# Filter convolution and SiLU layer: the first batch's products in rounds of two frequency pairs, with shared PSUM banks and two more groups in front of the second part

## Chip, cores and metric

One Trainium2 chip, one core, one launch. The metric is device time in microseconds (us), the median of the runs.

## The reference

```python
# batch 2, seq 12480, d_model 128, filter_order 64, d_ff 2048; all float32
h = maximum(pos_emb @ w1, 0) @ w2 * exp(-0.01 * pos)[:, None]     # the filter
u = x * v
y = irfft(rfft(u, 2*S) * rfft(h, 2*S))[:, :S]                     # causal convolution
a = (x * y).reshape(B*S, D)
g = a @ w_in;  out = (g * sigmoid(g)) @ w_out
```

## The kernel before

The transform is split by hand into two stages. A sequence is laid out as 98 x 64 points in two halves. Stage A turns the 98 points of a column into 98 frequencies by a matrix product; of these, frequencies come in 49 pairs q (NQ = 49). The second stage, for each pair, transforms over the 64 columns, multiplies by the filter's spectrum and transforms back, and its result `ws` goes to device memory (`wd`), from where tiles of tokens are loaded, transformed back over the 98 points (`yp`), multiplied with x (`ring`) and fed to the second part, the SiLU layer.

The kernel is scheduled by hand: each engine runs its instructions in the order in which the program writes them, and waits on what it reads. Its stretches:

- First stretch (string `seq`, a letter for each step): the filter's network, stage A of the filter (`Xh`) and of the first batch (`X`), the weights' conversion. The letters `f` and `B` load the first matrices and make the first filter products (`hp`).
- The loop over the 49 pairs (L661 to L694), first batch. For a pair q: `u_step` (L597) makes `up` on TensorE and ACT copies it, the halves exchanged, to `uw`. `hb_step` (L301) makes `hp`, the filter's transform of pair q + 3, which ACT copies to `zt`; `spectrum` (L321) makes `sps` of pair q + 1 from it, which ACT copies to `hab`. DVE multiplies `up` by parts of `hab` in place (`a_early`, `a_late`, with the temporary `at`), POOL does the like on `uw` (`b_step`, result `bt`), DVE adds both into `ps` (`s_step`). Two iterations later `w_step` (L645) makes `wps` from `ps`; ACT and DVE turn it into `ws` (`even_odd`), and SP stores it. `hab` is also stored (`hs`), for the second batch. `hp` has a PSUM pool of its own (`php`), `up` two buffers of one bank, `sps` and `wps` two banks each, whose halves two successive pairs use in turn.
- `side_steps` (L553), called in each iteration, does work beside the loop: it loads and splits the converted weights into high and low parts (L547 on ACT, L551 on DVE), loads and multiplies the first two groups of the second batch (L270 on POOL), and in iteration 47 loads further groups into `slots`.
- The bridge (string `seq3`): the last pairs' products, stage A of the second batch's first four groups (`stage_a_pairs`, L234: sixteen TensorE instructions into a tile `ap` of two banks, then four copies into X, all on ACT for `A`, on DVE for `a`), an activation table load, weight splits (`h`, `l`), the load of the first token tile (`L`) and its products (`Y`).
- The second part (from L961): the SiLU layer over 49 spans of tokens in 784 steps of six products, and beside it, paced by a counter, stage A of the remaining 28 groups of the second batch and then its products.

Of the kernel before, what the change touches and what calls it, by code (L numbers as in the profile page):

```python
# [31 lines left out]
NQ = R // 2  # L32
RE = 128
# [32 lines left out]
def moe_tiles():  # L66
# [15 lines left out]
    x47=2,  # L82
# [7 lines left out]
    seq3='smAumULASahhllhhllaxxrrrrYLxhhllhhll',  # L90
# [4 lines left out]
def kernel(  # L95
# [17 lines left out]
    fb0: bass.AP,  # L113
# [120 lines left out]
    def stage_a_pairs(g, psp, us, bufs, on_act):  # L234

        ap = psp.tile([128, 2, 512], F32, name=f"ap1_{g}", tag="ap", bufs=bufs)
        for k in range(4):
            for e in range(2):
                r = slice(64 * e, 64 * e + NQ)
                nc.tensor.matmul(ap[:, e, R * k : R * k + R], us[r, k], fe_sb[r], start=True, stop=True)  # L240
        for i in range(NI):
            for c in range(2):
                src = ap[64 * i : 64 * i + 64, :, 0 : 4 * R].rearrange("p e (d c q) -> p c q e d", c=2, q=NQ)
                dst = X[64 * c : 64 * c + 64, :, i * D + 4 * g : i * D + 4 * g + 4]
                dst = dst.rearrange("p (q e) d -> p q e d", e=2)
                if on_act:
                    nc.scalar.copy(out=dst, in_=src[:, c])
                else:
                    nc.vector.tensor_copy(dst, src[:, c])
# [44 lines left out]
    def load_fb(src, rp, q, bufs, e):  # L294
        t = rp.tile([128, 2, 2, 128], F32, name=f"fb{q}", tag="fb", bufs=bufs)
        e.dma_start(out=t, in_=src[q])
        return t

    fbs, zs, habs, prods = {}, {}, {}, {}

    def hb_step(q):  # L301

        if php is None:
            hp = psa.tile([128, 4, 256], F32, name=f"hp{q}", tag="ap", bufs=4)[:, 0]
            hp = hp.rearrange("p (k c n) -> p k c n", k=2, c=2)
        else:
            hp = php.tile([128, 2, 2, 64], F32, name=f"hp{q}", tag="hp", bufs=2)
        for k in range(2):
            for s in range(2):
                r = slice(64 * s, 64 * s + 64)  # L310
                nc.tensor.matmul(  # L311
                    hp[r, k].rearrange("p c k -> p (c k)"),
                    Xh[2 * q >= KA][:, 2 * q - (2 * q >= KA) * KA + k, r],
                    fbs[q][:, k, 0],
                    start=True,
                    stop=True,
                )
        zs[q] = rpa.tile([128, 2, 2, 64], F32, name=f"zt{q}", tag="zt", bufs=3)
        nc.scalar.copy(out=zs[q], in_=hp)

    def spectrum(q, hab):  # L321

        zt = zs.pop(q)
        sp = sps[:, :, q % 2]
        for m in range(2):
            for s in range(2):
                r = slice(64 * s, 64 * s + 64)
                for k in range(2):
                    nc.tensor.matmul(sp[64 * k : 64 * k + 64, s, m], zt[r, k, m], w2_sb[r], start=True, stop=True)  # L329
        nc.scalar.copy(out=hab.rearrange("p m s d -> p s m d"), in_=sp)  # L330
# [69 lines left out]
    php = None  # L400
    n_a = n_z = n_h = n_f = 0
# [9 lines left out]
    for t in P["seq"]:  # L411
# [35 lines left out]
        elif t == "|":  # L447
            early.release()
            xpool = pool("xpool")
            X = xpool.tile([128, R, NI * D], F32, name="X")  # L450
            rpa = pool("rp2a")
        elif t == "f":
            fbs[n_f] = load_fb(fb0, rpa, n_f, 4, nc.sync)
            n_f += 1
        elif t == "B":
            hb_step(len(zs))
# [7 lines left out]
    php = pool("php", space=PSUM, side="right")  # L464
# [57 lines left out]
    def even_odd(b, q, rp, wp, nb):  # L522

        p, tag, n = (rp, "ws", nb["ws"]) if b or q < NQ - 2 else (rp, "fb", 9)
        ws = p.tile([128, NI, 2, D], F32, name=f"ws{b}_{q}", tag=tag, bufs=n)
# [66 lines left out]
    nb = dict(up=2, uw=2, at=2, bt=2, ps=2, ws=2)  # L592

# [3 lines left out]
    def u_step(q):  # L597

        up = pp.tile([128, 2, NI, D], F32, name=f"up0_{q}", tag="up", bufs=nb["up"])
        for c in range(2):  # L600
            for k in range(2):
                nc.tensor.matmul(  # L602
                    up[64 * k : 64 * k + 64, c].rearrange("p i d -> p (i d)"),
                    fbs[q][:, k, 0, 64 * c : 64 * c + 64],
                    X[:, 2 * q + k],
                    start=True,
                    stop=True,
                )
        uw = rp.tile([128, 2, NI, D], F32, name=f"uw0_{q}", tag="uw", bufs=nb["uw"])
        nc.scalar.activation(out=uw[:, 0], in_=up[:, 1], func=AF.Copy, scale=-1.0)  # L610
        nc.scalar.copy(out=uw[:, 1], in_=up[:, 0])  # L611
        return up, uw

    def times_h(e, out, u, h):
        e.tensor_tensor(out=out, in0=u, in1=h.unsqueeze(1).broadcast_to([128, u.shape[1], D]), op=ALU.mult)  # L615

    def flat(t):
        return t.rearrange("p c i d -> p (c i) d")
# [4 lines left out]
    def a_early(q, up, hab):  # L623
        a2 = rp.tile([128, 2, D], F32, name=f"at{q}", tag="at", bufs=nb["at"])
        times_h(nc.vector, a2, up[:, :, 0], hab[:, 0, 1])
        return a2

    def a_late(up, hab, a2):
        times_h(nc.vector, flat(up), flat(up), hab[:, 0, 0])
        add(nc.vector, up[:, :, 1], up[:, :, 1], a2)  # L630

    def b_step(q, uw, hab):
        bt = rp.tile([128, 3, 2, D], F32, name=f"bt{q}", tag="bt", bufs=nb["bt"])
        b01 = bt[:, 0:2]
        times_h(nc.gpsimd, flat(b01), flat(uw), hab[:, 1, 0])
        times_h(nc.gpsimd, bt[:, 2], uw[:, :, 0], hab[:, 1, 1])
        add(nc.gpsimd, b01[:, :, 1], b01[:, :, 1], bt[:, 2])
        return b01

    def s_step(q):  # L640
        up, bt = prods[q]
        prods[q] = rp.tile([128, 2, NI * D], F32, name=f"ps{q}", tag="ps", bufs=nb["ps"])
        add(nc.vector, prods[q].rearrange("p c (i d) -> p c i d", i=NI), up, bt)

    def w_step(q):  # L645

        p, f = prods.pop(q), fbs.pop(q)
        wp = wps[:, :, q % 2]
        for c in range(2):
            for k in range(2):  # L650
                r = slice(64 * k, 64 * k + 64)
                nc.tensor.matmul(wp[:, k], f[r, c, 1], p[r, c], start=(c == 0), stop=(c == 1))  # L652
        wss[q] = even_odd(0, q, rp, wp.rearrange("p k (i d) -> p k i d", i=NI), nb)
        next(wss[q])

    def ws_step(q):
        for _ in wss.pop(q):
            pass

    wss = {}  # L660
    for it in range(-1, NQ):  # L661
        while n_f <= min(it + 6, NQ - 1):
            fbs[n_f] = load_fb(fb0, rp, n_f, 9, nc.sync if it < 0 else nc.scalar)
            n_f += 1
        q = it
        if 0 <= q < NQ:
            up, uw = u_step(q)
        q = it - 3
        if 0 <= q < NQ:
            ws_step(q)  # L670
        q = it
        if 0 <= q < NQ:
            a2 = a_early(q, up, habs[q])
        q = it - 1
        if 0 <= q < NQ:
            s_step(q)
        q = it + 3
        if 3 <= q < NQ:
            hb_step(q)
        q = it + 1  # L680
        if 0 <= q < NQ:
            hab = rp.tile([128, 2, 2, D], F32, name=f"hab{q}", tag="hab", bufs=3)
            spectrum(q, hab)
            habs[q] = hab
        q = it
        if 0 <= q < NQ:
            hab = habs.pop(q)
            a_late(up, hab, a2)
            prods[q] = up, b_step(q, uw, hab)
            nc.sync.dma_start(out=hs[q], in_=hab.rearrange("p m s d -> p (m s d)"))  # L690
        q = it - 2
        if 0 <= q < NQ:
            w_step(q)
        side_steps(it)  # L694

    pps.release()
    php.release()
    psa = pool("psa3", space=PSUM)
# [17 lines left out]
    def attn_tile(n, wt, xs, psp, tag):  # L716
# [3 lines left out]
        yp = psp.tile([128, 512], F32, name=f"yp{n}", tag=tag[0], bufs=tag[1])  # L720
# [34 lines left out]
    n_a = n_t = n_h = n_l = 0  # L755
    n_r = 4
    for t in P["seq3"]:
# [69 lines left out]
    def batch1_steps():  # L827
        for g in range(NA, D // 4):
            uv.mul(nc.gpsimd)
            yield P['ya']  # L830
            stage_a_pairs(g, psa, uss.pop(g), 1, True)
# [7 lines left out]
        def load_f(q):  # L839
            return load_fb(fb, rp, q, 2, nc.sync)  # L840
# [186 lines left out]
def _constants():  # L1027
# [23 lines left out]
    fb0 = np.stack([fwd, inv0], axis=1).reshape(NQ, 2, 2, 128, 128).transpose(0, 3, 1, 2, 4)  # L1051
# [5 lines left out]
    return {k: np.ascontiguousarray(a, dtype=np.float32) for k, a in dict(fa=fa, fs=fs, feo=feo, fe=fe, fb=fb, fb0=fb0, win=win).items()}  # L1057
# [56 lines left out]
```

## Time and profile before

| | |
|---|---|
| median of 3 runs | 1545.48 us (1542.5 to 1547.77) |
| the profiled execution | 1546.87 us, of which the trace spans 1545.0 |
| TensorE (PE) busy | 1514.3 us, 98% |
| VectorE (DVE) / ScalarE (ACT) / GpSimd (POOL) busy | 1227.3 / 990.2 / 633.5 us |
| chain that ended last | 91% on PE |
| first stretch, loop, bridge, second part | to 109.5, to 262.4, to 281.4, to 1545 us |

PE is the matrix engine, PEld its weight loads, SP the queue that issues most transfers. A busy PE is not one that streams at its peak: an instruction's record covers its latency too, and records overlap. So the order and the distance of the starts tell more than the busy share.

### The profile page before, as it was taken

The numbers are of one execution on the slowest core, as the hardware profiler recorded it, in microseconds if no ns is written. First come the engines' busy times: TensorE is split into PE (matmuls) and PEld (weight loads), VectorE is DVE, ScalarE is ACT, GpSimd is POOL, SyncE is SP. The second block draws the span as 40 slices with busy tenths as digits, with TensorE's granted clock in tenths as the row PEclk, the third lists the DMA queues.
The fourth block names the chain that finished last, engine by engine and source line by source line (L and its number), as shares of the span: only waits on it lengthen the run. The fifth ranks groups of instructions, "written<-read, shape, count | busy, mean of one in ns | idle before, by whom it ended". The sixth has DMA issues, their size and how long they took to land.

```text
span 1545.0 us, 31519 instructions
## 1 busy us (share of the span) xinstructions
PE 1514.3 (98%) x11732; PEld 1245.1 (81%) x11732; DVE 1227.3 (79%) x2138; ACT 990.2 (64%) x1910; POOL 633.5 (41%) x671
## 2 busy tenths in 40 slices
PE   8989998899999999999999999999999999999999
PEld 7976666787888888888888888888888888888887
DVE  5658898676799999999999987777777777777776
ACT  2545665677778788787887765555555555555554
POOL 3658888233378888888888730000000000000000
PEclk9999999799999999999999999999999999999999
DMA  8767787654354454544445521111111211111100
GB/s 238 215 211 240 254 291 243 197 167 145 99 150 137 132 148 143 143 137 142 142 142 155 147 89 38 46 47 40 47 41 47 62 34 46 54 33 47 53 30 14
DMA packets 115569, 184.84 MB, mean 120 GB/s; under 512 B 11058, under 2 KB 48984, under 8 KB 115416
## 3 DMA queue, kind: packets, MB, share of 16 engines
q1 hardware_dynamic: 101368, 158.45, 33.9%
q10 hardware_dynamic: 14048, 24.37, 4.8%
q8 instruction: 93, 1.52, 0.4%
q14 instruction: 60, 0.49, 0.1%
HBM read 129.37 MB, written 53.41 MB: 118 GB/s over the span
## 4 chain that ended last, share of the span: by engine, by line
PE 91%; DVE 3%; DMA 2%; ACT 1%; issue 1%; POOL 1%; ACTq 0%; SPq 0%; DVEq 0%; POOLq 0%
PE op L1001 12%; PE hq L968 11%; PE hq L969 11%; PE op L1002 11%; PE hq L970 11%; PE op L1003 11%; PE yp L727 4%; PE wps L652 3%; PE up L602 3%; PE ap L218 2%; PE wp L471 2%; PE aph L379 2%; PE ap L240 2%; PE up L471 2%; PE sps L329 2%; PE hp L311 1%
## 5 line engine op out<-in xcount | busy, mean ns | idle before, releaser
L975 ACT ACTIVATE g<-hq 128x512 f32<-128x512 f32 x424 | 253.9, 599 | 265.2 <-PE hq L970 237.4
L980 DVE TENSOR_TENSOR gl<-g,gh 128x512 fp32r<-128x512 f32 x424 | 293.6, 692 | 94.5 <-PE hq L970 65.8
L1001 PE MATMUL op<-gh,woh 128*128 128x512 f32 (+1 forms) x784 | 313.3, 400 | 0.0
L968 PE MATMUL hq<-ah,wih 128*128 128x512 f32 (+1 forms) x784 | 308.2, 393 | 2.0 <-ACT ah L749 1.3
L969 PE MATMUL hq<-al,wih 128*128 128x512 f32 (+1 forms) x784 | 306.1, 390 | 0.7 <-DVE al L751 0.7
L1002 PE MATMUL op<-gl,woh 128*128 128x512 f32 (+1 forms) x784 | 305.8, 390 | 0.0
L970 PE MATMUL hq<-ah,wil 128*128 128x512 f32 (+1 forms) x784 | 305.7, 390 | 0.0
L1003 PE MATMUL op<-gh,wol 128*128 128x512 f32 (+1 forms) x784 | 305.1, 389 | 0.0
L975 ACT ACTIVATE hq<-hq 128x512 f32<-128x512 f32 (+1 forms) x360 | 206.7, 577 | 95.2 <-PE hq L970 85.5
L980 DVE TENSOR_TENSOR gl<-hq,gh 128x512 fp32r<-128x512 f32 (+1 forms) x360 | 243.9, 683 | 22.5 <-ACT gh L979 13.5
L977 DVE CAST gh<-hq 128x512 fp32r<-128x512 f32 (+1 forms) x247 | 166.3, 673 | 41.7 <-ACT hq L975 41.2
L977 DVE CAST gh<-g 128x512 fp32r<-128x512 f32 x318 | 135.1, 425 | 72.1 <-ACT g L975 71.7
L968 PEld LDWEIGHTS hq<-ah,wih 128*128 128x128 f32 x784 | 147.9, 189 | 39.2 <-DVE gl L980 6.6
L970 PEld LDWEIGHTS hq<-ah,wil 128*128 128x128 f32 x784 | 148.0, 189 | 31.1
L969 PEld LDWEIGHTS hq<-al,wih 128*128 128x128 f32 x784 | 148.0, 189 | 30.3 <-DVE al L751 1.1
L1003 PEld LDWEIGHTS op<-gh,wol 128*128 128x128 f32 x784 | 147.5, 188 | 30.7
L1001 PEld LDWEIGHTS op<-gh,woh 128*128 128x128 f32 x784 | 147.7, 188 | 29.5 <-issue 0.2
L1002 PEld LDWEIGHTS op<-gl,woh 128*128 128x128 f32 x784 | 147.9, 189 | 24.3 <-DVE gl L980 0.3
L615 POOL TENSOR_TENSOR bt<-uw,hab 128x512 f32<-128x512 f32 x98 | 96.2, 1004 | 17.8 <-ACT uw L611 17.5
L727 PEld LDWEIGHTS yp<-feo_sb,slots 98*64 98x64 f32 x2048 | 64.9, 139 | 21.5 <-issue 17.7
L727 PE MATMUL yp<-feo_sb,slots 98*64 98x49 f32 (+1 forms) x2048 | 71.4, 225 | 3.3 <-DMA slots<-wd 3.3
L270 POOL TENSOR_TENSOR slots<-slots 128x512 f32<-128x512 f32 x30 | 39.0, 1300 | 84.6 <-DMA slots<-in_ve_dram 71.9
(1065 smaller groups left out, 2405.9 us busy)
## 6 DMA issues: line engine op xcount, KB each, us to landing
slots<-hs SPq DMA_DIRECT2D x98, 256.0 KB
slots<-wd SPq DMA_DIRECT2D x48, 490.0 KB
hs<-hab SPq DMA_DIRECT2D x49, 256.0 KB
wd<-ws SPq DMA_DIRECT2D x49, 256.0 KB
slots<-in_fb_dram SPq DMA_DIRECT2D x49, 256.0 KB
wd<-slots SPq DMA_DIRECT2D x49, 256.0 KB
out_dram<-ot ACTq DMA_DIRECT2D x48, 256.0 KB
fb<-in_fb_dram ACTq DMA_DIRECT2D x43, 256.0 KB
```

The lines of the kernel that those rows point to most:

```text
L471: nc.tensor.matmul(out[:, k].rearrange("p i d -> p (i d)"), f[:, k], a[:, k], start=(i == 0), stop=(i == len(passes) - 1),)
L615: e.tensor_tensor(out=out, in0=u, in1=h.unsqueeze(1).broadcast_to([128, u.shape[1], D]), op=ALU.mult)
L727: nc.tensor.matmul(yp[h : h + 64, a : a + k], wt[:, t, e * D + h : e * D + h + 64], feo_sb[:, e, 0:k], start=True, stop=True,)
L968: nc.tensor.matmul(hp[:, 0:w], wih[:, fs], ah[:, 0:w], start=True, stop=False)
L969: nc.tensor.matmul(hp[:, 0:w], wih[:, fs], al[:, 0:w], start=False, stop=False)
L970: nc.tensor.matmul(hp[:, 0:w], wil[:, fs], ah[:, 0:w], start=False, stop=True)
L975: nc.scalar.activation(out=g[:, 0:w], in_=hp[:, 0:w], func=AF.Silu)
L977: nc.vector.tensor_copy(gh[:, 0:w], g[:, 0:w])
L980: nc.vector.tensor_tensor(out=gl[:, 0:w], in0=g[:, 0:w], in1=gh[:, 0:w].bitcast(F32), op=ALU.subtract)
L1001: nc.tensor.matmul(o[:, 0:w], woh[:, fs], gh[:, 0:w], start=(f == 0), stop=False)
L1002: nc.tensor.matmul(o[:, 0:w], woh[:, fs], gl[:, 0:w], start=False, stop=False)
L1003: nc.tensor.matmul(o[:, 0:w], wol[:, fs], gh[:, 0:w], start=False, stop=(f == NF - 1))
```

## The change

The loop takes two pairs in one round (25 rounds, the last with one pair). Each tile of the loop is twice as large and most have one buffer instead of two or three; one vector instruction does for two pairs what two did, but the copies to `uw` and `hab`, and two of the products on POOL, stay one for a pair. The filter's products `hp` of the next round are written into one of the two banks of `sps`, in front of that round's `up`. The forward and inverse matrices are loaded separately (`ff`, `fi`). In the bridge six groups instead of four go through stage A, in turn into a tile of their own and into the buffers of `up`, one of them (`b`) with half of its copies on ACT and half on DVE; the second part has 26 groups left, four instead of two are loaded in iteration 47, and `side_steps` starts three iterations earlier.

```diff
-    x47=2,
+    x47=4,
-    seq3='smAumULASahhllhhllaxxrrrrYLxhhllhhll',
+    seq3='sbmULAmSamAmahhllhhllxxrrrrYLxhhllhhll',
@@ stage_a_pairs
-                if on_act:
+                if on_act[i]:
@@
+    def load_ff(r, e):
+        ffs[r] = rpa.tile([128, 2, 2, 128], F32, name=f"ff{r}", tag="ff", bufs=4)
+        e.dma_start(out=ffs[r], in_=ff[r])
+    def load_fi(r, e):
+        fis[r] = rp.tile([128, 2, 2, 128], F32, name=f"fi{r}", tag="fi", bufs=3)
+        e.dma_start(out=fis[r], in_=fi[r])
+    def qs(r):
+        return range(min(2, NQ - 2 * r))
-    def hb_step(q):
...
+    def hp_mm(hp, r, n):            # four products of pair 2r + n into hp
...
+    def zt_tile(r):
+        zs[r] = rpa.tile([128, 2, 2, 2, 64], F32, name=f"zt{r}", tag="zt", bufs=2)
+    def spectrum(r, hab):
+        zt = zs.pop(r)
+        for n in qs(r):
...
+                        nc.tensor.matmul(
+                            sps[64 * k : 64 * k + 64, s, n, m], zt[h, n, k, m], w2_sb[h], start=True, stop=True
+                        )
+        for n in qs(r):
+            nc.scalar.copy(out=hab[:, n].rearrange("p m s d -> p s m d"), in_=sps[:, :, n])
@@ side_steps
-        k = it - (KA // 2 + 1)
+        k = it - (KA // 2 - 2)
@@
+    def u_step(r):
+        up = pp.tile([128, 2, 2, NI, D], F32, name=f"up0_{r}", tag="up", bufs=2)
+        uw = rp.tile([128, 2, 2, NI, D], F32, name=f"uw0_{r}", tag="uw", bufs=1)
+        for n in qs(r):
...
+            nc.scalar.activation(out=uw[:, n, 0], in_=up[:, n, 1], func=AF.Copy, scale=-1.0)
+            nc.scalar.copy(out=uw[:, n, 1], in_=up[:, n, 0])
+    def a_step(r, up, hab):         # at has bufs=1
...
+        times_h(nc.vector, a2, up[:, :, :, 0], hab[:, :, 0, 1])
+        times_h(nc.vector, flat(up), flat(up), hab[:, :, 0, 0])
+        add(nc.vector, u1, u1, a2.rearrange("p n c d -> p (n c) d"))
+    def b_step(r, uw, hab):         # bt has bufs=2, b2 bufs=1
...
+        for n in range(w):
+            k = slice(n, n + 1)
+            times_h(nc.gpsimd, flat(bt[:, k]), flat(uw[:, k]), hab[:, k, 1, 0])
+        times_h(nc.gpsimd, b2, uw[:, :, :, 0], hab[:, :, 1, 1])
+        add(nc.gpsimd, b1, b1, b2.rearrange("p n c d -> p (n c) d"))
+    def s_step(r):                  # one addition for the round; ps has bufs=1
+    def w_step(r):                  # both pairs' products, one ACT copy to ws
+    def ws_step(r):                 # two DVE instructions, one store to wd
+    def ap_tile(g):
+        return (psa, "ap", 1) if g % 2 == 0 else (pp, "up", 2)
@@ the loop
+    for r in range(-1, NR):
+        # loads of ff (three rounds ahead) and fi (one ahead), on ACT's queue from r = 0
+        if r >= 2:
+            ws_step(r - 2)
+        if 1 <= r + 1 < NR:
+            hp = sps[:, 0].rearrange("p n m d -> p (n m d)").rearrange("p (n k c t) -> p n k c t", n=2, k=2, c=2)
+            for n in qs(r + 1):
+                hp_mm(hp[:, n], r + 1, n)
+            nc.scalar.copy(out=zt_tile(r + 1)[:, 0:w], in_=hp[:, 0:w])
+        if r >= 1:
+            s_step(r - 1)
+        if r >= 0:
+            up, uw = u_step(r)
+        if r + 1 < NR:
+            habs[r + 1] = rp.tile([128, 2, 2, 2, D], F32, name=f"hab{r + 1}", tag="hab", bufs=2)
+            spectrum(r + 1, habs[r + 1])
+        if r >= 0:
+            a_step(r, up, hab)
+            prods[r] = up, b_step(r, uw, hab)
+            # store of hab to hs
+        if r == NR - 1:
+            pps.release()
+            psa = pool("psa3", space=PSUM)
+            stage_a_pairs(0, *ap_tile(0), uss.pop(0), (True, True))
+        if r >= 1:
+            w_step(r - 1)
+        for it in (2 * r, 2 * r + 1):
+            if 0 <= it < NQ:
+                side_steps(it)
@@ the bridge
+    n_a = 1
+            on_act = {"A": (True, True), "a": (False, False), "b": (True, False)}[t]
+            stage_a_pairs(n_a, *ap_tile(n_a), uss.pop(n_a), on_act)
         elif t == "s":
+            s_step(NR - 1)
+            ws_step(NR - 2)
         elif t == "U":
+            w_step(NR - 1)
+            ws_step(NR - 1)
```

In the first stretch two matrices `ff` are loaded ahead and two pairs' `hp` made, where it was three of each.

## Rows read from the trace of the kernel before

**Rows 1.** Busy time by stretch: loop, bridge, second part while the side work lasts.

```profile
core 0: us, PE busy (x) PEld busy (x) DVE busy (x) ACT busy (x) POOL busy (x), PEclk, DMA share, GB/s
109.50:262.40 152.90, 149.03 (x1918) 100.66 (x1914) 135.31 (x292) 93.31 (x248) 133.06 (x146) 1.00 0.77 256
262.40:281.40 19.00, 11.20 (x129) 10.12 (x129) 11.81 (x25) 8.19 (x19) 6.82 (x7) 0.74 0.72 245
281.40:923.00 641.60, 639.05 (x4161) 529.99 (x4162) 563.37 (x915) 497.14 (x977) 435.85 (x467) 0.99 0.48 140
```

**Rows 2.** The chain that ended last, in the loop: start, us, what.

```profile
122.33 1.01 PE up L602 x8
...
125.44 1.01 PE up L602 x8
```

**Rows 3.** Timeline of TensorE about 201 us: start, us, engine, line, operation.

```profile
200.56 0.39 PE L602 MATMUL up<-X,fb 128*64 128x256 f32 x2
...
200.77 0.39 PE L602 MATMUL up<-X,fb 128*64 128x256 f32 x2
...
200.99 0.50 PE L311 MATMUL hp<-fb,Xhb 128*64 128x128 f32 x6
...
201.10 0.50 PE L311 MATMUL hp<-fb,Xhb 128*64 128x128 f32 x6
```

**Rows 4.** Groups by form, 110 to 262 us: busy us, mean ns | idle before.

```profile
L615 POOL TENSOR_TENSOR bt<-uw,hab 128x512 f32<-128x512 f32 x48 | 61.2, 1275 | 17.6 <-ACT uw L611 17.3
L621 POOL TENSOR_TENSOR bt<-bt 128x256 f32<-128x256 f32 x48 | 36.5, 760 | 3.8
...
L615 DVE TENSOR_TENSOR up<-up,hab 128x512 f32<-128x512 f32 x48 | 33.1, 690 | 0.0
...
L330 ACT COPY hab<-sps 128x512 f32<-128x512 f32 x49 | 28.7, 587 | 2.4
...
L615 DVE TENSOR_TENSOR at<-up,hab 128x256 f32<-128x256 f32 x48 | 20.3, 424 | 13.0 <-ACT uw L611 13.0
...
L610 ACT ACTIVATE uw<-up 128x256 f32<-128x256 f32 x49 | 18.8, 385 | 35.2 <-PE up L602 35.2
```

**Rows 5.** Timeline, last iterations of the loop, all engines; [idle before <-releaser].

```profile
249.02 0.42 DVE L615 TENSOR_TENSOR at<-up,hab 128x256 f32<-128x256 f32 x1 [0.23 <-ACT uw L611]
...
249.54 1.27 POOL L270 TENSOR_TENSOR spare<-spare 128x512 f32<-128x512 f32 x1
...
254.41 1.08 PE L602 MATMUL up<-X,fb 128*64 128x256 f32 x8 [0.78 <-DVE ps L621]
...
261.04 0.45 SPq L266 DMA_DIRECT2D slots<-in_ve_dram  x1
```

**Rows 6.** Timeline at the loop's start.

```profile
109.67 0.81 ACT L229 COPY X<-ap 128x784 f32<-128x784 f32 x1 [2.78 <-PE ap L218]
...
118.08 1.14 PE L652 MATMUL wps<-ps,fb 64*128 64x256 f32 x8
```

**Rows 7.** Timeline, from the last `ws` to the second part's first product.

```profile
270.94 0.42 DVE L530 TENSOR_TENSOR ws<-wps,ws 128x256 f32<-128x256 f32 x1
...
281.38 0.69 PE L968 MATMUL hq<-ah,wih 128*128 128x384 f32 x1 [1.31 <-ACT ah L749]
```

**Rows 8.** Timeline, stage A of the second batch's first group.

```profile
263.31 1.06 PE L240 MATMUL ap<-fe_sb,spare 49*128 49x98 f32 x16
...
264.41 1.96 ACT L247 COPY X<-ap 64x392 f32<-64x392 f32 x4 [0.49 <-PE ap L240]
```

**Rows 9.** Timeline: a weight split on DVE beside POOL's addition.

```profile
200.86 0.42 DVE L551 TENSOR_TENSOR wil<-spare,wih 128x256 fp32r<-128x256 f32 x1
200.94 0.92 POOL L621 TENSOR_TENSOR bt<-bt 128x256 f32<-128x256 f32 x1
```

**Rows 10.** Busy time by short stretch about the bridge's end, columns as in rows 1.

```profile
271.50:274.95 3.45, 2.21 (x34) 1.90 (x32) 2.25 (x4) 3.18 (x5) 0.00 (x0) 0.99 0.33 97
274.95:278.40 3.45, 0.71 (x14) 0.71 (x16) 2.85 (x7) 1.44 (x6) 0.00 (x0) 0.50 1.01 317
...
292.00:295.43 3.43, 3.43 (x14) 2.99 (x14) 1.11 (x2) 1.72 (x4) 1.42 (x2) 0.50 0.46 149
```

More of the change, by code (lines that the diff above doesn't have):

```diff
@@ L32 @@
 NQ = R // 2
+NR = (NQ + 1) // 2
 RE = 128
@@ L112 @@
     fb: bass.AP,
-    fb0: bass.AP,
+    ff: bass.AP,
+    fi: bass.AP,
     win: bass.AP,
@@ L232, in stage_a_halves, with stage_a_pairs @@
         yield
-    def stage_a_pairs(g, psp, us, bufs, on_act):
-        ap = psp.tile([128, 2, 512], F32, name=f"ap1_{g}", tag="ap", bufs=bufs)
+    def stage_a_pairs(g, psp, tag, bufs, us, on_act):
+        ap = psp.tile([128, 2, 512], F32, name=f"ap1_{g}", tag=tag, bufs=bufs)
         for k in range(4):
@@ L317, in hb_step @@
                 )
[L318 to L330, printed above, removed]
+    def zt_tile(r):
+        zs[r] = rpa.tile([128, 2, 2, 2, 64], F32, name=f"zt{r}", tag="zt", bufs=2)
+        return zs[r]
+    def spectrum(r, hab):
+        zt = zs.pop(r)
+        for n in qs(r):
+            for m in range(2):
+                for s in range(2):
+                    h = slice(64 * s, 64 * s + 64)
+                    for k in range(2):
+                        nc.tensor.matmul(
[3 more added lines that the diff above has]
+            nc.scalar.copy(out=hab[:, n].rearrange("p m s d -> p s m d"), in_=sps[:, :, n])
     nc.vector.memset(w1_sb, 0.0)
@@ L452 @@
         elif t == "f":
-            fbs[n_f] = load_fb(fb0, rpa, n_f, 4, nc.sync)
+            if n_f < 2:
+                load_ff(n_f, nc.sync)
             n_f += 1
         elif t == "B":
-            hb_step(len(zs))
+            if n_b < 2:
+                hp = psa.tile([128, 4, 256], F32, name=f"hp{n_b}", tag="ap", bufs=4)[:, 0]
+                hp = hp.rearrange("p (k c n) -> p k c n", k=2, c=2)
+                hp_mm(hp, 0, n_b)
+                nc.scalar.copy(out=(zs[0] if n_b else zt_tile(0))[:, n_b], in_=hp)
+            n_b += 1
     for q, n in ((zq, n_z - 2 * NP), (zw, 0), (hq_, n_h - NJ // 4), (aq, n_a - D // 4)):
@@ L522, in even_odd @@
     def even_odd(b, q, rp, wp, nb):
[L524 to L525 removed]
+        ws = rp.tile([128, NI, 2, D], F32, name=f"ws{b}_{q}", tag="ws", bufs=nb["ws"])
         we, wo = ws[:, :, 0], ws[:, :, 1]
@@ L591 @@
     pps = pool("pps", space=PSUM)
-    nb = dict(up=2, uw=2, at=2, bt=2, ps=2, ws=2)
     sps = pps.tile([128, 2, 2, 2, D], F32, name="sps")
     wps = pp.tile([128, 2, 2, 256], F32, name="wps")
[L597 to L611, printed above, removed]
+    def u_step(r):
+        up = pp.tile([128, 2, 2, NI, D], F32, name=f"up0_{r}", tag="up", bufs=2)
+        uw = rp.tile([128, 2, 2, NI, D], F32, name=f"uw0_{r}", tag="uw", bufs=1)
+        for n in qs(r):
+            for c in range(2):
+                for k in range(2):
+                    nc.tensor.matmul(
+                        up[64 * k : 64 * k + 64, n, c].rearrange("p i d -> p (i d)"),
+                        ffs[r][:, n, k, 64 * c : 64 * c + 64],
+                        X[:, 2 * (2 * r + n) + k],
+                        start=True,
+                        stop=True,
+                    )
+            nc.scalar.activation(out=uw[:, n, 0], in_=up[:, n, 1], func=AF.Copy, scale=-1.0)
+            nc.scalar.copy(out=uw[:, n, 1], in_=up[:, n, 0])
@@ L612, in u_step @@
         return up, uw
     def times_h(e, out, u, h):
-        e.tensor_tensor(out=out, in0=u, in1=h.unsqueeze(1).broadcast_to([128, u.shape[1], D]), op=ALU.mult)
+        n, c = u.shape[1], u.shape[2]
+        e.tensor_tensor(out=out, in0=u, in1=h.unsqueeze(2).broadcast_to([128, n, c, D]), op=ALU.mult)
     def flat(t):
-        return t.rearrange("p c i d -> p (c i) d")
+        return t.rearrange("p n c i d -> p n (c i) d")
     def add(e, out, a, b):
         e.tensor_tensor(out=out, in0=a, in1=b, op=ALU.add)
[L623 to L658, printed above, removed]
-    wss = {}
[L661 to L694, printed above, removed]
@@ L696 @@
-    pps.release()
-    php.release()
-    psa = pool("psa3", space=PSUM)
+    def a_step(r, up, hab):
+        w = len(qs(r))
+        up, hab = up[:, 0:w], hab[:, 0:w]
+        a2 = rp.tile([128, 2, 2, D], F32, name=f"at{r}", tag="at", bufs=1)[:, 0:w]
+        times_h(nc.vector, a2, up[:, :, :, 0], hab[:, :, 0, 1])
+        times_h(nc.vector, flat(up), flat(up), hab[:, :, 0, 0])
+        u1 = up[:, :, :, 1].rearrange("p n c d -> p (n c) d")
+        add(nc.vector, u1, u1, a2.rearrange("p n c d -> p (n c) d"))
@@ new lines, in b_step @@
+    def b_step(r, uw, hab):
+        w = len(qs(r))
+        bt = rp.tile([128, 2, 2, NI, D], F32, name=f"bt{r}", tag="bt", bufs=2)[:, 0:w]
+        b2 = rp.tile([128, 2, 2, D], F32, name=f"b2{r}", tag="b2", bufs=1)[:, 0:w]
+        uw, hab = uw[:, 0:w], hab[:, 0:w]
+        for n in range(w):
+            k = slice(n, n + 1)
+            times_h(nc.gpsimd, flat(bt[:, k]), flat(uw[:, k]), hab[:, k, 1, 0])
+        times_h(nc.gpsimd, b2, uw[:, :, :, 0], hab[:, :, 1, 1])
+        b1 = bt[:, :, :, 1].rearrange("p n c d -> p (n c) d")
+        add(nc.gpsimd, b1, b1, b2.rearrange("p n c d -> p (n c) d"))
+        return bt
@@ new lines, in s_step @@
+    def s_step(r):
+        up, bt = prods[r]
+        ps = prods[r] = rp.tile([128, 2, 2, NI * D], F32, name=f"ps{r}", tag="ps", bufs=1)
+        w = len(qs(r))
+        f = "p n c i d -> p (n c i d)"
+        add(nc.vector, ps[:, 0:w].rearrange("p n c m -> p (n c m)"), up[:, 0:w].rearrange(f), bt.rearrange(f))
+    def w_step(r):
+        p, f = prods.pop(r), fis.pop(r)
+        for n in qs(r):
+            for c in range(2):
+                for k in range(2):
+                    h = slice(64 * k, 64 * k + 64)
+                    nc.tensor.matmul(wps[:, k, n], f[h, n, c], p[h, n, c], start=(c == 0), stop=(c == 1))
+        w = len(qs(r))
+        ws = wss[r] = rp.tile([128, 2, NI, 2, D], F32, name=f"ws0_{r}", tag="ws", bufs=2)
+        nc.scalar.copy(
+            out=ws[:, 0:w, :, 1].rearrange("p n i d -> p (n i) d"),
+            in_=wps[:, 1, 0:w].rearrange("p n (i d) -> p (n i) d", d=D),
+        )
@@ new lines, in ws_step @@
+    def ws_step(r):
+        w = len(qs(r))
+        ws = wss.pop(r)
+        we, wo = (ws[:, 0:w, :, e].rearrange("p n i d -> p (n i) d") for e in range(2))
+        w0 = wps[:, 0, 0:w].rearrange("p n (i d) -> p (n i) d", d=D)
+        nc.vector.tensor_tensor(out=we, in0=w0, in1=wo, op=ALU.add)
+        nc.vector.tensor_tensor(out=wo, in0=w0, in1=wo, op=ALU.subtract)
+        nc.sync.dma_start(
+            out=wd[0][2 * r : 2 * r + w].rearrange("q c t i e d -> (c t) q (i e d)"),
+            in_=ws[:, 0:w].rearrange("p n i e d -> p n (i e d)"),
+        )
@@ new lines, in ap_tile @@
+    def ap_tile(g):
+        return (psa, "ap", 1) if g % 2 == 0 else (pp, "up", 2)
+    wss = {}
+    n_ff, n_fi = 2, 0
+    for r in range(-1, NR):
+        while n_ff <= min(r + 3, NR - 1):
+            load_ff(n_ff, nc.sync if r < 0 else nc.scalar)
+            n_ff += 1
+        while n_fi <= min(r + 1, NR - 1):
+            load_fi(n_fi, nc.sync if r < 0 else nc.scalar)
+            n_fi += 1
+        if r >= 2:
[4 more added lines that the diff above has]
+                hp_mm(hp[:, n], r + 1, n)
+            w = len(qs(r + 1))
+            nc.scalar.copy(out=zt_tile(r + 1)[:, 0:w], in_=hp[:, 0:w])
[7 more added lines that the diff above has]
+        if r >= 0:
+            hab = habs.pop(r)
+            a_step(r, up, hab)
+            prods[r] = up, b_step(r, uw, hab)
+            w = len(qs(r))
+            nc.sync.dma_start(
+                out=hs[2 * r : 2 * r + w].rearrange("q p n -> p q n"),
+                in_=hab[:, 0:w].rearrange("p n m s d -> p n (m s d)"),
+            )
+        if r == NR - 1:
[7 more added lines that the diff above has]
+                side_steps(it)
@@ L719, in attn_tile @@
         w = sum(ws)
-        yp = psp.tile([128, 512], F32, name=f"yp{n}", tag=tag[0], bufs=tag[1])
+        yp = psp.tile([128, 1024] if tag[0] == "up" else [128, 512], F32, name=f"yp{n}", tag=tag[0], bufs=tag[1])
         o = 0
@@ L839, in load_f @@
         def load_f(q):
-            return load_fb(fb, rp, q, 2, nc.sync)
+            t = rp.tile([128, 2, 2, 128], F32, name=f"fb{q}", tag="fb", bufs=2)
+            nc.sync.dma_start(out=t, in_=fb[q])
+            return t
         def load_h(q):
@@ L1050, in _constants @@
     inv0 = inv.reshape(NQ, 2, 2, 64, 128).transpose(0, 2, 1, 3, 4).reshape(2 * NQ, 128, 128)
-    fb0 = np.stack([fwd, inv0], axis=1).reshape(NQ, 2, 2, 128, 128).transpose(0, 3, 1, 2, 4)
+    ff, fi = (
+        np.concatenate([a.reshape(NQ, 2, 128, 128), np.zeros((1, 2, 128, 128))])
+        .reshape(NR, 2, 2, 128, 128)
+        .transpose(0, 3, 1, 2, 4)
+        for a in (fwd, inv0)
+    )
     fb = np.stack([fwd, inv], axis=1).reshape(NQ, 2, 2, 128, 128).transpose(0, 3, 1, 2, 4)
```

40 lines of the change are left out of this document (11 added, 29 removed).

## Prediction

> **What bounds the kernel now.** I read the table of busy time by stretch first. The first batch's loop (109.5 to 262.4 us) and the second part (from 281.4) keep TensorE busy nearly throughout; between them lies a bridge of 19 us in which it works 11.2, at a mean granted clock of 0.74 [rows 1]. The change touches all three, so each is priced by itself.
>
> Then the chain that ended last, inside the loop: it goes from TensorE to TensorE, and `up` comes back every 3.11 us [rows 2]. So TensorE sets the iteration. But does it stream all that time? Narrow pieces of TensorE's timeline show instructions starting in pairs: 0.215 us apart for `up` (200.56, 200.77, then `hp` at 200.99) and 0.11 for `hp` [rows 3]. An iteration has four pairs of `up`, four of `hp`, four quadruples of `sps` (128 columns as `hp`, so I take 0.11 each) and four pairs of `wps` (256 columns as `up`, 0.215 each): 4 x (0.215 + 0.11 + 0.11 + 0.215) = 2.60. The other 0.51 us lie at the three places where the array's shape changes: 128x64 for `up` and `hp`, 64x64 for `sps`, 64x128 for `wps`. These are what a round of two pairs can halve.
>
> **The loop.** A round needs 2 x 2.60 + 0.51 = 5.71 us of TensorE, where two iterations take 6.22. It keeps three shape changes, since `hp` now stands next to `up` in the same shape. From the groups by form, the others' work for a round: on DVE 0.424 for 256 elements and 0.690 for 512 give 1.22 for 1024 by the same slope, so `at` 0.69, `up` 1.22, its addition 0.69, two of `ws` 1.38, `ps` 1.22: 5.2. ACT: four `uw` of 0.385 (they keep their size), `zt` 0.59, two `hab` of 0.587, `ws` 0.59: 3.9. POOL: 1.275 for each of three 512-element products and 1.27 for a 512-element addition (that of the like-sized multiplication of [rows 5]; 0.760 is the row for 256): 5.1 [rows 4]. All are below 5.71, so no engine's sum becomes the bound.
>
> The waits are closer. `uw`, `at`, `ps`, `b2`, `sps` and `wps` now have one buffer each. Put w(r-1) at 0: it lasts 1.92 (eight pairs, 1.72, and 0.2 of the 0.51), hp(r+2) starts at 1.92, u(r+1) at 2.95, sp(r+2) at 4.67, w(r) at 5.71.
> First ring: w(r-1) done at 2.0, ACT copy to 2.6, two of `ws` on DVE to 4.0, `ps` to 5.2, and w(r) may start at about 5.4. 0.3 to spare.
> Second ring: the first half of u(r+1) done at 3.98 (0.86, and 0.17 by which a record of 0.39 outlasts the next start), two ACT copies to 4.75, POOL to 9.85, `ps` to 11.07, w(r+1) at 11.2; TensorE comes there at 11.42. 0.2 to spare.
> Third: `at` starts only when ACT has finished with `up`, as before (the wait on `uw`, [rows 5]); that is 5.6, `up` and its addition end at 8.2, and the next `ws` is due at 8.3. 0.1 to spare.
> Behind a late w stand the next hp and u on TensorE, and behind a late `ps` on DVE the whole of `at`. With margins of 0.1 to 0.3 I take 5.8 rather than 5.71 for a round; the ends are 5.71 (all hidden) and 6.05 (the second ring late by 0.7, as if POOL waited for both halves of `uw`).
>
> The shared banks speak against the change: hp(r+2) may be written only when ACT has emptied the spectrum of r+1. sp ends at 5.7 of the frame before, that is 0.0; two `hab` copies end at 1.15, and hp comes at 1.92. Covered by w, 0.77 to spare. If w is late, so is hp: no second price.
> The Trainium skill ("PSUM — Partial Sum Buffer", PSUM bank collisions) wants two engines kept off one bank and quadrant, even for reads alone. The DVE row that waits for ACT's reading agrees; without the rule `at` could start some 0.75 us earlier, and the third margin would be 0.8 instead of 0.1.
>
> **Fill.** Before, the last copy into X ends at 110.48 and the first `wps` starts at 118.08 [rows 6]. Now hp(1) stands in front of u(0) and shares its banks with sp(0), so it waits for two `hab` copies that ACT makes after that X copy: 110.48 + 1.2 = 111.7; hp(1) to 112.7, half of u(0) 113.7, ACT 114.5, POOL 119.6, `ps` 120.8, w(0) at 121.0. That costs 2.9 us against before, though it carries two pairs.
>
> **Work beside the loop.** POOL's two `spare` multiplications (1.27 each) cost TensorE 0.78 in one iteration before [rows 5]. Now they fall into two consecutive rounds in which POOL has 0.7 idle: 2 x 1.27 - 2 x 0.7 - 0.2 = 0.9 late. Two weight splits a round (DVE 0.42 each, five rounds) overrun the third margin by little: 0.4 in all. ACT issues two loads a round as before; SP's eight X loads of the second batch (twice as many) stand before the last `wd` writes, but take 8 x 0.45 = 3.6 us of issuing [rows 5], and the next `wd` write is that long off: its `ws` ends 4.0 after w(22) begins.
>
> **The end of the loop.** w(22) starts at T = 121.0 + 22 x 5.8 + 1.3 = 249.9. From there the products run without cover: w(22), ACT, two `ws`, `ps` 5.3; w(23), ACT, two `ws` to 9.4; w(24), single, 10.5; ACT 0.37 and two `ws` of 0.42: T + 11.8 = 261.7. Before, the same last `ws` ends at 271.36 [rows 7]. So 9.7 us earlier.
> What follows is unchanged: the writes land, the first token tile is loaded, `yp`, `ring`, the first product of the second part at 281.38, 10.0 after that `ws` [rows 7]. Groups 2 to 5 must fit into these 10 us. Two groups more than before mean 2 x 1.06 on TensorE, and a group's four copies, some 2 us [rows 8], once more on ACT and once more on DVE, in a stretch of 19 us in which TensorE worked 11.2, ACT 8.2 and DVE 11.8 [rows 1]. I take 0, with 2 us (one group's copies in front of `ring`) as the bad end.
>
> **The second part.** It is TensorE's all the way, so two groups fewer save what they cost there: 1.06 of their own [rows 8] and a shape change of 0.17 (0.51 / 3): 2 x 1.2 = 2.4. Bounds: 2.1 and, if the shape change costs 0.5, 3.1.
>
> **Sum.** -9.7 - 2.4 = -12.1 on the profiled execution's 1546.87 us, which lies 1.39 above the median of the runs: 1534.8 there, 1533.4 against the median of 1545.48. No change by less than 0.3% (4.6 us) can be told from none.
>
> **Rivals.**
> 1. Late products. The rings' margins are used up, a round takes 6.05 and w waits on `ps` each time. For it: the margins are made of extrapolated durations. Against: nothing in the steady loop waits so now. 22 x 0.25 = 5.5 more: 1539.
> 2. The half of `up`. The second half of u is held until ACT has read the first half, as if the tile were one bank. Price a round: 0.17 + 0.77, 0.95 on top of 5.71. 22 x (6.66 - 5.8) = 19: 1552, slower. It makes the kernel slower by 0.3% from a stall of 0.9 a round. For it: `at` is held in just that way today [rows 5]. Against: the halves lie in different banks, and `at` touches the one that ACT reads.
> 3. POOL bound. One `bt` addition took 0.92 beside a weight split [rows 9], against a mean of 0.76 [rows 4]; if the long POOL instructions all ran 1.26 times as long, a round would be 6.4 and nothing of the 1.27s hidden: 22 x 0.62 + 1.6 = 15 more: 1548. Against: it is 0.92 only where a split runs.
> The Trainium skill ("SBUF — State Buffer", Who interferes with whom) says that a DVE instruction with two SBUF inputs contends with GpSimd's reads; of this loop's instructions only the split has two, so by that rule the slow case stays in five rounds. The two rows agree.
> 4. It doesn't do what it says: the 0.51 us are waits for data that come with each pair, and a round takes 6.22. 22 x 0.42 = 9: 1542. Against: the gaps lie at the shape changes.
> 5. The clock. TensorE had full clock until 274.95, having worked 2.21 of the last 3.45 us; then half clock, working 0.71 of 3.45; and it still had half clock at 292 to 295, when it was busy all the time [rows 10]. From 281.4 to 295.4 that costs 7 us. With two more groups in the bridge the clock may stay up: 1526. Against: its idle stretches (7.8 us of the bridge, [rows 1]) don't vanish.
> 6. The bridge overruns: A copies hold `ring`: 2 to 4 us more, 1536.
>
> **How the numbers follow.** Forecast 0.55 (its own range 1529 to 1537), late products 0.18, half of `up` 0.06, POOL 0.04, no saving 0.05, clock 0.08, bridge 0.04. Faster: forecast, clock, bridge and most of the late products, 0.82. Same: the rest of those, POOL, no saving, 0.12. Slower: half of `up`, 0.06. The range from 1526 to 1542 leaves out the slower case, POOL's and half of the clock's and of the no-saving case: under 0.2.
>
> **What would show it.** In the chain after, `up` returns every 5.7 to 5.8 us, `hp` and `up` adjoin, and no TensorE wait on `ps` stands inside the loop. A wait of `wps` on `ps` in each round means rival 1 (look whether POOL or ACT comes before it), a gap between the halves of `up` rival 2, POOL without idle time rival 3. The first product of the second part should come near 271.5. If it does and the end doesn't follow, the second part ate it, and the granted clock after that point is to be read first.

## The result, and the profile after

The changed kernel is slower by 0.7%: 1555.38 us, the median of 4 runs (1554.48 to 1556.43), against 1544.3 for the kernel before beside it (1542.5 to 1547.77); ratio 1.0069, 95% interval 1.0049 to 1.009. The profiled execution took 1556.43 us, of which the trace spans 1554.6, 9.6 more than before (the medians differ by 11.1). Where do they arise? First busy time by stretch. The first row covers the stretch that the loop took before, though the loop now goes on to 276.5; the others are the bridge and the second part (before: [rows 1]).

```profile
core 0: us, PE busy (x) PEld busy (x) DVE busy (x) ACT busy (x) POOL busy (x), PEclk, DMA share, GB/s
109.50:262.40 152.90, 132.16 (x1820) 93.07 (x1816) 117.01 (x138) 81.59 (x187) 113.88 (x90) 1.00 0.72 242
276.50:295.60 19.10, 13.26 (x144) 12.48 (x144) 12.41 (x25) 10.13 (x22) 8.10 (x9) 0.69 0.78 267
295.60:937.00 641.40, 638.91 (x4159) 531.39 (x4160) 566.11 (x920) 494.15 (x973) 432.21 (x465) 0.99 0.47 140
```

In the first row every engine now works less: TensorE 132 of 153 us where it was 149, DVE 117 where it was 135. That isn't an engine that became the bound, it is waiting. The chain that ended last shows it (start, us, what; before: [rows 2]):

```profile
188.46 0.38 ACT uw L620
189.16 1.08 PE up L613 x8
190.24 1.03 PE sps L335 x32
191.28 1.93 PE wps L670 x16
193.20 1.02 PE sps L315 x16
194.23 0.89 PE up L613 x8
195.22 0.38 ACT uw L620
195.92 1.08 PE up L613 x8
```

A round, from one second half of `up` to the next, takes 195.92 - 189.16 = 6.76 us, and the chain leaves TensorE once: between the two halves of `up` it goes through ACT's copies to `uw`. The table of waits from 112 to 262 us (engine and line, waited for: us in total, times, longest) says how often:

```profile
PEld up L613 <- ACT uw L621: 28.3, 22, 1.4
DVE at L626 <- ACT uw L621: 28.2, 18, 7.2
PE up L613 <- ACT uw L621: 18.3, 22, 1.0
```

22 times, 0.83 us each on TensorE; a wait of the products of `wps` on `ps` is not in that table. The timeline has one such round:

```profile
202.26 0.37 ACT L621 COPY uw<-up 128x256 f32<-128x256 f32 x1
202.68 1.08 PE L613 MATMUL up<-X,ff 128*64 128x256 f32 x8 [0.83 <-ACT uw L621]
```

The second half's products write other addresses of `up`, in the other bank, and still start only after ACT's last read of the first half.

What surrounds the loop: the start, and the last `ws` and first product of the second part (before: [rows 6, 7]).

```profile
110.35 0.81 ACT L231 COPY X<-ap 128x784 f32<-128x784 f32 x1 [2.78 <-PE ap L220]
112.57 1.09 PE L315 MATMUL sps<-ff,Xha 128*64 128x128 f32 x16 [1.24 <-ACT hab L339]
115.28 1.08 PE L613 MATMUL up<-X,ff 128*64 128x256 f32 x8 [0.75 <-ACT uw L621]
...
123.42 2.00 PE L670 MATMUL wps<-ps,fi 64*128 64x256 f32 x16
...
284.95 0.42 DVE L684 TENSOR_TENSOR ws<-wps,ws 128x256 f32<-128x256 f32 x1
...
295.61 0.69 PE L1006 MATMUL hq<-ah,wih 128*128 128x384 f32 x1 [1.89 <-ACT ah L786]
```

The last `ws` ends 14.0 us later than before and the first product comes 14.2 later; from there to the end it is 1259.0 us instead of 1263.6. So the loop loses 14 and the second part gives 4.6 back.

### The profile page after: what moved, and what is told of

Its sections match the earlier page's. It is cut to its first block, busy times and chain, and to the rows that moved or that the text cites. A ratio compares the mean times of both kernels' runs of the same rounds, so it can differ in the third digit from the quotient of the medians.

```text
span 1554.6 us, 30963 instructions
## 1 busy us (share of the span) xinstructions
PE 1506.3 (97%) x11732; PEld 1244.4 (80%) x11732; DVE 1225.9 (79%) x1995; ACT 982.6 (63%) x1862; POOL 622.9 (40%) x623
## 3 DMA queue, kind: packets, MB, share of 16 engines
q8 instruction: 92, 1.51, 0.4%
## 4 chain that ended last, share of the span: by engine, by line
PE 91%; DVE 4%; ACT 2%; DMA 1%; issue 1%; ACTq 0%; POOL 0%; SPq 0%; DVEq 0%; POOLq 0%
PE op L1039 12%; PE hq L1006 11%; PE hq L1007 11%; PE hq L1008 11%; PE op L1040 11%; PE op L1041 11%; PE yp L764 4%; PE wps L670 3%; PE up L613 3%; PE aph L388 2%; PE ap L220 2%; PE wp L484 2%; PE up L484 2%; PE ap L242 2%; PE sps L335 2%; PE sps L315 1%
## 5 line engine op out<-in xcount | busy, mean ns | idle before, releaser
L626 POOL TENSOR_TENSOR bt<-uw,hab 128x512 f32<-128x512 f32 x49 | 62.4, 1273 | 41.1 <-ACT uw L621 41.1
L509 POOL TENSOR_TENSOR slots<-slots 128x512 f32<-128x512 f32 x49 | 64.3, 1312 | 19.6 <-ACT slots L503 19.3
```

Source lines behind the costliest of these rows:

```text
L509: e.tensor_tensor(out=t[:, 0:2].rearrange("p k (i d) -> p k i d", i=NI), in0=u, in1=hab[:, :, m, 0].unsqueeze(2).broadcast_to([128, 2, NI, ...
L626: e.tensor_tensor(out=out, in0=u, in1=h.unsqueeze(2).broadcast_to([128, n, c, D]), op=ALU.mult)
```

## The experiments

Theory: the second half of `up` waits because both halves are one tile; the program guards the tile as a whole (an engine that touches any part of it waits for what another engine does in any other part), and nothing in the chip asks for it. Rivals: the arrangement of two pairs cannot run faster (the 0.51 us are no shape changes, or the rings are too tight); or the time lies in the bridge with its six groups.

**All products first.** In `u_step` both halves are issued to TensorE before the first copy is issued to ACT, by a loop of their own.

```diff
+        for n in qs(r):
             nc.scalar.activation(out=uw[:, n, 0], in_=up[:, n, 1], func=AF.Copy, scale=-1.0)
             nc.scalar.copy(out=uw[:, n, 1], in_=up[:, n, 0])
```

> The changed kernel with all products of a round's `up` ahead of the four ACT copies. Theory (the second half of `up` waits for ACT's reading of the first half because both stand in one tile): the wait inside `up`, 0.83 us of TensorE a round, goes, and the round falls from 6.76 us to 5.8 to 6.1 (not lower, since POOL now starts only when both halves are made, about 0.9 us later; then `wps` waits for `ps`). 22 rounds by 0.7 to 0.95: 15 to 21 us less than the changed kernel's 1555, so 1534 to 1540. Rival (the products of a round are late and hold TensorE whatever the order of `up`): the round stays at 6.5 to 6.8 with a wait of `wps` on `ps` instead, 1550 to 1556.

Measured: 1542.43 us (1539.01 to 1543.34), ratio to before 0.9974 (0.9963 to 0.9985). One added line is worth 13 us, less than the 15 to 21 expected. The wait moved; its timeline:

```profile
153.51 1.90 PE L613 MATMUL up<-X,ff 128*64 128x256 f32 x16
...
155.53 0.39 ACT L621 ACTIVATE uw<-up 128x256 f32<-128x256 f32 x1 [1.22 <-PE up L613]
...
156.95 2.00 PE L671 MATMUL wps<-ps,fi 64*128 64x256 f32 x16 [0.51 <-DVE ps L633]
```

`up` runs through, but now ACT's first copy starts after all sixteen products (153.51 + 1.90), though the half that it reads was done some 0.9 earlier: the same guard, in the other direction. POOL gets its first `uw` that much later, and `wps` waits for `ps`. Two rounds take 12.0 us here (`wps` at 144.95, 150.66 and 156.95: 5.71 and 6.29 in turn), so a round takes the 6.0 expected, and the rival's wait is there too, though a smaller one. Rounds with weight splits take up to 7.1.

**Two tiles.** `up` as two tiles of one bank each, same order on TensorE and ACT; DVE takes one instruction for a pair, since none can span two tiles. The bridge's groups share one tile `ap`.

```diff
-        up = pp.tile([128, 2, 2, NI, D], F32, name=f"up0_{r}", tag="up", bufs=2)
+        ups = [pp.tile([128, 2, NI, D], F32, name=f"up{n}_{r}", tag=f"u{n}", bufs=2) for n in qs(r)]
...
-        return (psa, "ap", 1) if g % 2 == 0 else (pp, "up", 2)
+        return (psa, "ap", 1)
```

> The changed kernel with `up` as two tiles of one bank each, instructions on TensorE and ACT in the same order as in the changed kernel; DVE's work on `up` is one instruction a pair again, and the bridge's groups take one tile in turn, so that only the loop is compared. Theory (the wait belongs to the common tile, not to the chip's need): no wait between the halves, a round of 5.7 to 5.9 us. Rival (the second half needs what ACT does in between): the round stays at 6.76. DVE's sum grows to about 5.8 us a round by the rows of one instruction each, so a round of 5.8 to 6.0 with DVE never idle would still be the theory.

Measured: 1542.02 us in one run. Its chain in the loop:

```profile
140.62 1.73 PE up L613 x16
142.34 1.03 PE sps L335 x32
143.38 1.93 PE wps L673 x16
145.31 1.02 PE sps L315 x16
146.33 1.73 PE up L613 x16
```

5.71 us a round, and no wait left on this chain. ACT copies the first half while TensorE writes the second:

```profile
146.16 1.90 PE L613 MATMUL up<-X,ff 128*64 128x256 f32 x16
147.32 0.38 ACT L620 ACTIVATE uw<-up 128x256 f32<-128x256 f32 x1 [0.36 <-PE up L613]
147.60 0.37 ACT L621 COPY uw<-up 128x256 f32<-128x256 f32 x1
```

So the stall is a matter of the tile. The last `ws` ends at 262.76, and yet the first product comes only at 280.45: with one `ap` the groups of the bridge follow one another, and what the loop saved is given back there:

```profile
264.56 2.03 PE L242 MATMUL ap<-fe_sb,slots 49*128 49x98 f32 x16 [2.09 <-ACT X L249]
269.07 2.03 PE L242 MATMUL ap<-fe_sb,slots 49*128 49x98 f32 x16 [2.48 <-DVE X L251]
```

**hp between the halves.** The tile stays, and the wait is covered: the filter's products of the next round run while ACT copies.

```diff
             nc.scalar.copy(out=uw[:, n, 1], in_=up[:, n, 0])
+            if n == 0:
+                hp_step(r)
```

> The changed kernel with the eight `hp` products moved between the two halves of `up`; the wait stays, but TensorE has 0.88 us of work of the same shape to cover it. Theory: the wait falls from 0.83 us to 0.1 or less, the round to 5.75 to 5.9 us; 22 rounds by 0.9: some 19 us less than the changed kernel, 1535 to 1538. POOL keeps its early start, so it should be as fast as the version with all products first, or faster. Rival (late products): 6.5 us or more, 1550.

Measured: 1537.87 us (1534.07 to 1541.01), ratio 0.9952 (0.9936 to 0.9968), as expected. It was run once more beside the last two runs below:

> The run with hp between the halves of `up` once more, unchanged, on the chip of the other two, so that they are compared with it there: rounds of 5.89 us, first product near 275, 1537.9 timed, ratio 0.995.

1538.81 us (1536.52 to 1540.14), ratio 0.9959 (0.9946 to 0.9973). Its first product comes at 279.2, not near 275; its last copy into X ends at 112.7 instead of 108.6, so the 4.1 us lie in the first stretch of the same kernel, and from the first `wps` to the first product both take 157.1. A first product is therefore best compared from the first `wps` on. A round of the first of the two runs, 5.89:

```profile
144.07 1.01 PE up L613 x8
145.09 0.87 PE sps L315 x16
145.96 1.04 PE up L613 x8
147.00 1.03 PE sps L335 x32
148.03 1.93 PE wps L680 x16
149.96 1.01 PE up L613 x8
```

Moving one call removes 0.87 of the 1.05 us.

**hp apart, in the kernel before.** `hb_step` behind `spectrum`, so that an iteration has four shape changes instead of three. It prices a change by itself.

```diff
-        q = it + 3
-        if 3 <= q < NQ:
-            hb_step(q)
         q = it + 1
...
             habs[q] = hab
+        q = it + 3
+        if 3 <= q < NQ:
+            hb_step(q)
```

> The kernel before with one thing moved: `hp` stands behind `sps` instead of between `up` and `sps`, so an iteration has four changes of the array's shape instead of three, and no other work is added. Theory (a change of shape costs TensorE about 0.17 us): the iteration grows from 3.11 to about 3.28 us, the whole by 49 x 0.17 = 8 us. Rival (the 0.51 us an iteration that do not stream are waits for data): the iteration stays at 3.11, within 2 us.

Measured: 1549.21 us in one run; `up` returns in its chain after

```profile
142.84 1.01 PE up L602 x8
...
146.10 1.01 PE up L602 x8
```

3.26 us instead of 3.11: 0.15 for a shape change, where the prediction had 0.51 / 3 = 0.17. The table of waits over these iterations has no wait of TensorE's products for data. The whole kernel is only 3.9 us longer than the kernel before beside it (1545.29), not 8: a single run, in which, beside the profile of before, the first stretch ends 2.6 us earlier and the second part is 1.1 shorter. From the first `wps` to the first product it is 5.9 longer (169.2 against 163.3).

**Two tiles, and two for the bridge.** As the two tiles, in a pool of their own that is released after the last `up`; the bridge's odd groups then use two tiles there.

```diff
+    ppu = pool("ppu", space=PSUM, side="right")
...
-        return (psa, "ap", 1)
+        return (psa, "ap", 1) if g % 2 == 0 else (psb, "apa" if g == 3 else "apb", 1)
...
             s_step(NR - 1)
+            ppu.release()
+            psb = pool("psb", space=PSUM, side="right")
```

> The rounds with the two one-bank tiles again, now in a pool that is released after the last `up` of the first batch, so that the groups between the two parts have two tiles in turn for what they hand from TensorE to ScalarE, as in the kernel before. Theory (the wait belongs to the one tile over two banks, and the long way from the last `ws` to the first product in the run with two tiles came of the single tile that its groups of the second batch shared): rounds of 5.71 us, last `ws` at about 262.8 as in the run with two tiles, first product of the second part some 10 to 10.5 us later, at about 273, and 1259.5 us from there to the end as in the three runs with six groups in front: about 1532.5 profiled, some 1534 timed, ratio about 0.993. Rival: the groups between the parts take their 12 us anyway, because the clock is at half speed there or because more of them are left over when the rounds end earlier; then the first product stays near 280 and the time near 1541, no better than the run with two tiles.

Measured: 1535.95 us (1533.48 to 1538.06), ratio 0.9942 (0.9929 to 0.9956), the lowest median of all; the interval overlaps that of hp between the halves on the same chip. The theory holds within 2 us: rounds of 5.71, last `ws` at 264.07, first product at 274.36, 1258.7 from there to the end. The profiled span, 1533.1, is 11.9 below that of the kernel before.

**Four groups.** The run with hp between the halves, with four groups in front of the second part as before.

```diff
-    x47=4,
+    x47=2,
-    seq3='sbmULAmSamAmahhllhhllxxrrrrYLxhhllhhll',
+    seq3='sbmULAmSahhllhhllxxrrrrYLxhhllhhll',
```

> The run with hp between the halves of `up`, with four groups of the second batch in front of the second part in place of six, as in the kernel before; all else as in that run. This prices the moved groups by themselves. Theory (two groups less in front cost the second part about what the six-group runs gain over the kernel before from the first product to the end, 3 to 4 us, and the stretch before gives back less, since the rounds hide the side work): first product 0 to 1 us earlier than 275.1, 1262.5 us from there to the end instead of 1259.4, so 1537 to 1538 profiled and about 1540 timed, 2 to 3 us more than with six. Rival: each group in front lengthens the stretch ahead of the first product by as much as it shortens what follows; then first product near 272 and the same time as with six, near 1537.

Measured: 1539.71 us (1536.49 to 1541.55), ratio 0.9965 (0.9951 to 0.9978), beside 1538.81 with six on the same chip: a difference too small to be told from none. In the traces from the first `wps` to the first product it is 154.7 us with four and 157.1 with six, from there to the end 1262.1 and 1259.1. Two groups in front cost 2.4 and save 3.0. The theory is wrong where it took the two groups in the bridge to cost next to nothing (0 to 1 us); the rival is nearer. So the moved groups explain neither the loss of the changed kernel nor the gain of the others.

## Why the prediction was wrong

**The step that failed** is the one on which the round of 5.8 rests: that the halves of `up` are independent. It stood as the second rival, was priced at 0.95 us a round and 1552 us, and got a chance of 0.06 because "the halves lie in different banks". That argument is about the chip, and the wait isn't the chip's: the same products and copies overlap as soon as each half is a tile. What spoke for it was in the rows of before: `at`, a reader, waits for ACT, another reader of the same tile [rows 5]. I explained this by the bank that both touch. In that kernel a tile of `up` is one bank, so its rows can't tell a guard of the tile from a rule of the bank; I chose the bank, and so stopped at its border. The Trainium skill ("PSUM — Partial Sum Buffer", PSUM bank collisions) says that the compiler's scheduler adds a dependency between engines on the same bank and quadrant. Here one is held across two banks, so the measurement goes further than the page; with the page's dependencies alone the round would be 5.71.

The size: 6.76 - 5.71 = 1.05 us a round, of which 0.83 is the wait in the table; the rest is that the next half no longer follows inside the latency of the one before. With 6.76 for 5.8 in the prediction's own sum, 22 x 0.96 = 21.1 on top of -12.1 gives +9.0; the span grew by 9.6. That the two agree so well is in part luck: from the first `wps` to w(22) the loop is 19.2 us over the 128.9 predicted (the stalls hid the 1.3 of side work), the fill and the end of the loop are 1.7 and 2.1 over, the first stretch ends 0.7 later, and the second part is 2.2 under.

**Right, once the halves are apart.** The 0.51 us as three shape changes: 5.71 measured against 5.71 computed, and 0.15 for a fourth. The Trainium skill ("TensorEngine Tiling (Array Packing)", Key Properties) says that a change of the tiling mode drains TensorE and gives no time for it; the runs agree in that each change costs time. The second ring: with the copies behind all products a round takes 6.0, near the 6.05 of the late-products rival. The fill: `wps` 10.25 us after X's last copy in the run with two tiles for the bridge, 10.5 predicted; in the changed kernel 12.26, with two stalls of the halves in it.

**Mis-sized, and hidden by each other.** The profiled execution of the run with two tiles for the bridge comes near the forecast (-11.9 against -12.1), but not by its terms: the first product comes 7.0 earlier, not 9.7 (the first stretches end within 0.2 us of each other), and the second part gives 4.9, not 2.4. By the medians on its chip it is 8.9 faster (1535.95 against 1544.83); of the two profiled executions compared, this one lies below its median and that of before above.

- Side work: the five rounds with weight splits take 31.0 us there, 2.45 more than five of 5.71, where I had 0.4. Most other rounds take 5.71, below my 5.8, so the loop as a whole still takes 128.3 from the first `wps` to w(22), 128.9 predicted. In the first of the five a split takes 1.44 us beside POOL's addition. In the three of 6.24 each of the two splits takes 0.42, and it is DVE that has no time left:

```profile
160.55:166.26 5.71, 5.71 (x85) 4.26 (x81) 5.54 (x12) 3.54 (x8) 5.01 (x5) 1.00 0.71 250
196.02:202.26 6.24, 5.78 (x80) 4.26 (x81) 6.07 (x13) 4.06 (x11) 5.03 (x5) 1.00 0.87 287
...
199.53 0.75 DVE L564 TENSOR_TENSOR wil<-spare,wih 128x256 fp32r<-128x256 f32 x2
```

  DVE (third of the busy times) works 5.54 us in a round without splits, one instruction for each pair, and 6.07 in one of 6.24 with two; the chain stays on it from one `ps` (195.29) to the next (201.52). My own rows said as much: 5.2 and two splits of 0.42 are 6.04, more than 5.8. Where DVE takes both pairs in one instruction, a split can also be the longer one beside POOL; [rows 9] show only POOL longer. The changed kernel's timeline has both:

```profile
207.09 0.41 DVE L562 TENSOR_TENSOR wil<-spare,wih 128x256 fp32r<-128x256 f32 x1
207.11 1.53 POOL L632 TENSOR_TENSOR bt<-bt,b 128x512 f32<-128x512 f32 x1
...
207.69 1.23 DVE L562 TENSOR_TENSOR wil<-spare,wih 128x256 fp32r<-128x256 f32 x1 [0.19 <-ACT wih L558]
```

  The first split comes before POOL's addition, which takes 1.53 instead of 1.28; the second comes after it, takes 1.23 instead of 0.41 and ends at 208.92, 0.28 after the addition. In the changed kernel the stalled rounds had room for it (6.76 to 6.79). With hp between the halves the first split of a round takes 0.92 to 1.16, and the five rounds take 31.5 instead of 29.45.
- End of the loop: the last `wps` starts 10.25 us after w(22), 9.4 predicted, and the last `ws` ends 15.2 after it, 11.8 predicted. These 3.4 us outweigh the 1.0 by which the loop's last rounds come early, and are why the first product's gain is 2.7 short:

```profile
259.13 1.87 PE L676 MATMUL wps<-ps,fi 64*128 64x256 f32 x8 [1.76 <-ACT X L251]
...
262.78 0.37 ACT L679 COPY ws<-wps 128x256 f32<-128x256 f32 x1 [4.42 <-PE ap L244]
```

  Those eight products take 1.87 us where they took 1.13 in the changed kernel: the granted clock is at its lower level (0.50 of full speed) from 259.4; TensorE worked 2.36 of the 4.00 us from 255 to 259. And ACT's copy is put down to the products of a group behind them. Why it waits for these, no run tells.
- Second part: two groups fewer are 3.0 (four against six on one chip), near the prediction's upper bound of 3.1. After the first product the clock stays at its lower level for 14.0 us in the kernel before, 12.2 in the changed one and 12.3 in the fastest; 1.7 to 1.8 us less at half speed are another 0.9. The remaining 0.7 to 1.0 is less than what profiles with the same second part differ by (1262.1 to 1263.6 with four groups in front, three kernels).
- The bridge: two groups at 0 were 2.4, a little beyond the bad end of 2. The clock rival did not happen: in every run the lower level lasts past the first product.
- Two figures of the rivals don't follow from their rows, without changing the outcome: 1552 is 0.4% above 1545.48, not 0.3%; and 0.92 against 0.76 is a factor of 1.21, not 1.26, so POOL's round would be 6.2, not 6.4.

## What to carry to other kernels

When tiles are merged to save instructions, ask of each merged tile which other engine touches it while it is being written, and read the trace for what is guarded: if two readers of one tile wait for each other today, a writer of its other half may wait tomorrow, even in another bank. Split the tile where two engines overlap, or place other work between the halves; merge where one engine has it to itself. And an edit that makes rounds tighter takes away the cover of all side work: add that work to the sum of its engine, compare it with the new round, and take the longest row of it that the trace has, not the shortest.

## What the runs showed of the hardware

- A DVE subtraction of two SBUF inputs that starts while POOL adds ends only after POOL, though the tensors are not shared: 0.41 us alone, 0.92 to 1.51 when most of it falls beside POOL's addition (changed kernel, hp between the halves, two tiles for the bridge). It ends 0.27 to 0.28 after POOL's in the three places compared (201.91 after 201.64, 208.92 after 208.64, and in the fastest run 187.80 after 187.53); POOL's addition that comes second takes 1.53 to 1.55 instead of 1.28. The Trainium skill ("SBUF — State Buffer", Who interferes with whom) says that a DVE instruction with two SBUF inputs contends with a GpSimd instruction that reads SBUF, and that the order of issue decides who blocks. The trace agrees, both ways.
- A change of the array's shape costs TensorE 0.15 us (one more in an iteration, 3.11 to 3.26) to 0.17 us (0.51 for three) in a stream of such products.
